# A new hand-written order for gated linear attention and a maxout layer, and four zero fills on another engine

## The chip, the cores and the metric

The kernel runs on one core of one Trainium2 chip, in one launch. The metric is the device time of one execution in microseconds. The engines of the core are TensorE (PE, matrix products and transposes), VectorE (DVE), ScalarE (ACT), GpSimd (POOL) and SyncE (SP, which only issues transfers here).

## The reference

Everything is in float32; the weights come as 64-bit floats. `x`, 3072 x 384, is the result of the attention, and the output has the same shape.

```python
# q, k, v, a_re, a_im: (4, 8, 768, 48), batch x heads x positions x width
mag = sqrt(a_re * a_re + a_im * a_im)
scale = minimum(mag, 0.999) / (mag + 1e-06)
a_re_n, a_im_n = a_re * scale, a_im * scale
for t in range(768):
    new_re = a_re_n[t] * S_re - a_im_n[t] * S_im     # each row of the 48 x 48 state has its decay
    new_im = a_re_n[t] * S_im + a_im_n[t] * S_re
    S_re, S_im = new_re + outer(k[t], v[t]), new_im
    y[t] = q[t] @ S_re
x = y.transpose(0, 2, 1, 3).reshape(3072, 384)
h = maximum(maximum(x @ w1, x @ w2), x @ w3)         # 384 -> 768
out = h @ w_out                                      # 768 -> 384
```

## The kernel before

**Tiles.** The 768 positions are cut into 12 groups of 64 (`g` = 0 to 11). A group holds four batches, as two tiles `x` and `y` of two batches each: 128 partitions and 8 heads x 48 = 384 columns a tile. The products of the decays inside a group are formed as exponentials of summed logarithms and angles, so that a group's attention is a handful of matrix products; only the 48 x 48 states go from a group to the next.

**Stages of a group.** Each stage is a *step*, named `step:g`; where x, y or a digit stands behind the name it is for one tile or one part.
- Loads: `Lr`, `Li` (real and imaginary part of the decay), `Lk`, `Lq`, `Lv`.
- Decay: `sqr` and `sqi` square (ACT), `add` adds (DVE), `lnL`, `expw`, `expe`, `lne`, `relu`, `lnw`, `expL` (ACT), `xor`, `half`, `mulai`, `mulw`, `stt`, `turn` (DVE), `atan` (ACT), the magnitude `abs`, and the additions `Lnop` and `addw`, which from group 1 and 2 on are transfers that add into their destination, issued by POOL. In group 0 these steps are done in two halves (`add0`, `add1`).
- Sums along the group: `cs` and `sums` (PE), then `t`, `nf`, `Cd`, the magnitude `af`, the sines `sa`, `sb`, and the exponentials `En`, `Ek`, `Eq` (ACT).
- Keys and queries: `mk`, `mq`, `uk`, `uq` multiply on DVE into the tiles `uk0` to `uk2` and `uq0`, `uq1` (128 x 8 x 112 columns, of which 16 of each head stay zero); `tpk`, `tpq` are transposes on PE, `Kc`, `Qc` copy their results out of PSUM, `F` and `f0` to `f3` are small factors, `Q1`, `Q2`, `KB`, `QB`, `QG`, `kEn` scale on DVE.
- Scores and state: `A`, `B` (PE), the masked copies `g0` to `g3` (DVE) and `b0`, `b1` (ACT), then `y` (the result) and `dk` (the new state, PE), `h0`, `h1` (DVE), and `xx`, `xy`, which copy the result out.
- The layer behind it: `U11`, `U01`, `U12`, `U02` are products with the three weight matrices (PE, 256 columns for a group), `u11` to `u02` copy or take the maximum; `S`, `P`, `r` and `o` are the product with `w_out` in a form with seven products a pair of blocks, with the product of `w1` and `w_out` folded in; `D` stores.
- Once only: twelve weight blocks, loaded as pairs of integers (`WL`) and decoded to float32 by `Wa` (ACT), `Wb`, `Wc`, `We`, `Wf` (DVE) and `Wg` (an addition); `T`, `t`, `M`, `m` form the folded product; `Zf`, `Zg`, `Zh`, `Z2` to `Z4` and `CL` fill constants.

**The order.** `SCHEDULE` is a list of 1750 such steps, written out by hand, and `run` issues a step's instructions. Nothing is reordered afterwards: `Bound` ties every instruction of an engine behind the one before it on that engine, so the list is each engine's queue, and an instruction that waits holds up all that follow on its engine. The decays of group g+1 or g+2 are thus worked on between the scores of group g and the projection of group g-1. As all instructions are issued through `Bound`, the profile gives them all one line, L198, and they are told apart by the names of their tiles.

**The rooms.** PSUM is used as four rooms of two banks. `SLOTS` is a string of 258 digits: the n-th product that asks for a room gets the one that the n-th digit names, and waits until the reader of the product before it there is done.

**The second engine.** `OTHER` is a set of steps that a second engine does:

```python
def copy(out, in_):          # Kc, Qc, xx, xy: ACT, or DVE
def magnitude(out, in_):     # abs, af: ACT by a table, or DVE by a mask of the bits
def increase(out, in_):      # Lnop, addw, Wg: a POOL transfer that adds, or DVE
(pool if other() else sp).dma_start(...)   # Lk, Lq, Lv: SP's queue, or POOL's
```

and two of the maxima of the layer (`u01`, `u11`) go from ACT to DVE by it.

**The start.** Ahead of the list the first loads are issued and ACT loads its first table of functions. Then ACT fills the parts that stay zero of `uk0`, `uk1`, `uq0` and `uq1`, by multiplying a constant by 0 (lines 1030 and 1031), and DVE those of two `vb` tiles.

Of the kernel before, what the change touches and what calls it, by code (L numbers as in the profile page):

```python
# [22 lines left out]
relu0:0 xor1:0 Lix:1 xor0:0 Lnop0:0 abs0:0 Fx:0 Wa0:0 Wb0:0 half0:0 lnL1:0 expe1:0 expw1:0 lne1:0 Lkx:0 relu1:0 WL3:0
Wc0:0 We0:0 Lnop1:0 Wf0:0 pw0:0 Wa3:0 abs1:0 Wb3:0 half1:0 f3x:0 lnw0:0 Wc3:0 WL6:0 We3:0 f2x:0 expL0:0 mulai0:0 Liy:1
mulw0:0 stt0:0 pw1:0 Lrx:1 Lry:1 f1x:0 Zh:0 Wa6:0 Wb6:0 f0x:0 lnw1:0 expL1:0 mulai1:0 WL9:0 Lqx:0 mulw1:0 sumsx:0
atan0:0 Wf3:0 sqi:1 stt1:0 turn0:0 csx:0 sqr:1 atan1:0 WL10:0 Wc6:0 Eqx:0 tx:0 WL11:0 add:1 We6:0 Wa9:0 turn1:0 Ekx:0
# [10 lines left out]
Lqy:1 mulw:2 We7:0 Cdx:1 WL8:0 U02x:0 b1y:0 u02x:0 Wa8:0 yy:0 xy:0 sb:1 dky:0 stt:2 atan:2 h1y:0 sa:1 Wg5:0 Wf7:0
Wb8:0 U01y:0 turn:2 Wc8:0 mkx:1 U11y:0 u01y:0 u11y:0 U12y:0 Eky:1 Eny:1 mqx:1 ukx:1 U02y:0 Eqy:1 cs:2 sqi:3 uqx:1
tpqx:1 u02y:0 u12y:0 Z2:0 Lvy:1 Wg7:0 Z4:0 tpkx:1 Qcx:1 mqy:1 U21y:0 U21x:0 Lvy:2 u21y:0 We8:0 Wf8:0 Wg8:0 mky:1 Kcx:1
Q1x:1 Q2x:1 U22y:0 sumsx:2 kEnx:1 u22y:0 t:2 u21x:0 nfy:2 uqy:1 Eqx:2 Enx:2 F:2 nfx:2 Ekx:2 Ax:1 tpqy:1 f3:2 f0:2  # L40
uky:1 g0x:1 g1x:1 QBx:1 Oy:0 KBx:1 J3:0 af:2 f2:2 f1:2 Qcy:1 g2x:1 Lqx:2 mqx:2 Lvx:1 tpky:1 Q2y:1 dkx:1 QGx:1 sb:2
g3x:1 sa:2 uqx:2 Q1y:1 Lrx:3 Kcy:1 Bx:1 b1x:1 U12x:0 h0x:1 h1x:1 Lry:3 oy:0 U22x:0 b0x:1 tpqx:2 Lky:2 u12x:0 sqr:3
Qcx:2 KBy:1 Ay:1 QBy:1 u22x:0 sumsy:2 add:3 Lkx:2 g0y:1 g1y:1 g2y:1 g3y:1 Lqy:2 Eky:2 By:1 Lvx:2 yx:1 mky:2 QGy:1
kEny:1 lnL:3 xor:3 expw:3 QBx:2 xx:1 Ox:0 Eqy:2 mkx:2 Lry:4 Dy:0 expe:3 ukx:2 uky:2 b0y:1 Q1x:2 relu:3 Lrx:4 abs:3
lne:3 Lnop:3 addw:3 J1:0 Eny:2 Lqx:3 b1y:1 mqy:2 yy:1 half:3 Cdy:2 Lix:4 Cdx:2 xy:1 Liy:4 lnw:3 expL:3 J2:0 mulai:3
Lkx:3 tpky:2 kEny:2 Kcy:2 tpkx:2 Kcx:2 Lky:3 U11:1 uqy:2 u11:1 mulw:3 U01:1 tpqy:2 stt:3 atan:3 sqr:4 ox:0 h0y:1 dky:1
Q2x:2 turn:3 sqi:4 add:4 KBx:2 sumsx:3 u01:1 Qcy:2 h1y:1 cs:3 Ekx:3 h0y:2 lnL:4 Ax:2 Q2y:2 Enx:3 t:3 relu:4 kEnx:2
g0x:2 Eqx:3 Lix:5 g1x:2 nfy:3 U12:1 g2x:2 nfx:3 u12:1 g3x:2 S3:1 expw:4 U02:1 h0x:2 dky:2 af:3 F:3 expe:4 abs:4 addw:4
mqx:3 sb:3 Q1y:2 u02:1 S1:1 h1y:2 Bx:2 Lqy:3 sa:3 S2:1 Lry:5 Lvy:3 f2:3 Ay:2 b0x:2 g0y:2 P5:1 g1y:2 g2y:2 f0:3 J4:0
QBy:2 S4:1 b1x:2 P1:1 f1:3 f3:3 lnw:4 P7:1 g3y:2 QGx:2 P6:1 r1:1 sumsy:3 KBy:2 expL:4 Dx:0 r6:1 Eky:3 dkx:2 r5:1 r7:1  # L50
r57:1 Eny:3 h1x:2 By:2 yx:2 Lrx:5 xor:4 mkx:3 QGy:2 mky:3 b1y:2 ukx:3 Px:1 lne:4 Lnop:4 Eqy:3 Py:1 mqy:3 mulai:4 h0x:3
P4:1 uqy:3 uqx:3 half:4 Cdx:3 b0y:2 uky:3 P3:1 Lkx:4 Cdy:3 P2:1 xx:2 sqr:5 yy:2 xy:2 tpkx:3 Kcx:3 tpqx:3 Qcx:3 mulw:4
stt:4 U01:2 Lkx:5 Q2x:3 oy:1 Lqy:4 atan:4 Q1x:3 turn:4 ox:1 u01:2 tpky:3 QBx:3 Kcy:3 tpqy:3 F:4 Lqx:4 kEny:3 Qcy:3
QGx:3 Q1y:3 Q2y:3 sumsx:4 cs:4 f3:4 h0y:3 Liy:5 t:4 nfx:4 Ekx:4 Eqx:4 Enx:4 KBx:3 nfy:4 sqi:5 f2:4 U11:2 add:5 Ax:3
Bx:3 f0:4 Dx:1 u11:2 f1:4 lnL:5 g0x:3 mkx:4 Lvy:4 sb:4 Ay:3 mqx:4 g1x:3 af:4 g2x:3 U02:2 g0y:3 sa:4 g1y:3 g3x:3 ukx:4
relu:5 u02:2 g2y:3 Lvx:3 uqx:4 S3:2 g3y:3 KBy:3 U12:2 u12:2 b0x:3 expe:5 expw:5 kEnx:3 Lqx:6 lne:5 tpkx:4 tpqx:4 Lvx:4
dky:3 Kcx:4 S1:2 Qcx:4 dkx:3 Lky:4 sumsy:4 Eqy:4 h1y:3 S2:2 xor:5 Lry:6 Lnop:5 P1:2 Dy:1 abs:5 Eky:4 QBy:3 Lix:6 P7:2
mqy:4 P6:2 b1x:3 h1x:3 addw:5 half:5 Lrx:6 yx:3 mky:4 By:3 Eny:4 uqy:4 Cdx:4 Px:2 Py:2 lnw:5 expL:5 mulai:5 b0y:3
uky:4 Liy:6 P5:2 mulw:5 QGy:3 r1:2 xx:3 r6:2 b1y:3 S4:2 kEnx:4 P4:2 P2:2 r5:2 Cdy:4 sqr:6 sqi:6 P3:2 stt:5 atan:5
tpqy:4 Lqx:5 r7:2 r57:2 add:6 tpky:4 Qcy:4 yy:3 ox:2 dkx:4 Lix:7 Kcy:4 sumsx:5 h0x:4 turn:5 Lrx:7 Dx:2 xor:6 oy:2 xy:3  # L60
h1x:4 Q1y:4 lnL:6 Enx:5 sumsy:5 Eky:5 Ekx:5 Q1x:4 relu:6 mkx:5 cs:5 t:5 U11:3 nfx:5 expw:6 Eqx:5 Q2y:4 nfy:5 expe:6
Lky:5 mky:5 u11:3 abs:6 kEny:4 Eny:5 U01:3 af:5 Q2x:4 half:6 QGx:4 Lry:7 u01:3 Ax:4 Cdy:5 h0y:4 g0x:4 Eqy:5 g1x:4
mqx:5 dky:4 Cdx:5 F:5 g2x:4 U12:3 h1y:4 sb:5 KBx:4 QBx:4 sa:5 uqx:5 Lqy:5 U02:3 f3:5 f2:5 g3x:4 ukx:5 u12:3 uky:5
addw:6 tpqx:5 f0:5 tpky:5 u02:3 lnw:6 expL:6 f1:5 Qcx:5 Ay:4 mulai:6 Bx:4 P1:3 lne:6 Liy:7 S1:3 P5:3 mulw:6 S2:3 b1x:4
Kcy:5 g0y:4 KBy:4 b0x:4 Dy:2 sqi:7 P6:3 QBy:4 g1y:4 g2y:4 g3y:4 By:4 Lvx:5 Lky:6 mqy:5 yx:4 r1:3 S3:3 stt:6 b1y:4 P7:3
uqy:5 atan:6 tpkx:5 b0y:4 tpqy:5 QGy:4 Kcx:5 r6:3 turn:6 yy:4 Qcy:5 r5:3 r7:3 Lnop:6 sqr:7 Q1x:5 xy:4 Lkx:6 Lvy:5
h0x:5 S4:3 Q2y:5 sumsx:6 xx:4 kEnx:5 r57:3 cs:6 t:6 Ekx:6 add:7 nfy:6 Q1y:5 Py:3 nfx:6 lnL:7 P4:3 expw:7 Px:3 U01:4
QGx:5 expe:7 kEny:5 relu:7 Eqx:6 QBx:5 mqx:6 Enx:6 P2:3 af:6 Q2x:5 dkx:5 h1x:5 Liy:8 KBx:5 u01:4 sa:6 mkx:6 abs:7
sumsy:6 Eny:6 F:6 Lry:8 addw:7 oy:3 Lqy:6 U11:4 Eqy:6 P3:3 f2:6 Dy:3 f0:6 h0y:5 Eky:6 f3:6 f1:6 Bx:5 xor:7 u11:4 QBy:5
ox:3 lnw:7 sb:6 Ax:5 KBy:5 Ay:5 mqy:6 By:5 half:7 g0x:5 g1x:5 g2x:5 g3x:5 g0y:5 g1y:5 g2y:5 U02:4 Lvx:6 lne:7 b1x:5  # L70
b0x:5 yx:5 g3y:5 u02:4 expL:7 Lrx:8 mulai:7 U12:4 b1y:5 mulw:7 stt:7 Cdx:6 Lix:8 b0y:5 xx:5 atan:7 ukx:6 S3:4 P7:4
QGy:5 P1:4 tpkx:6 Kcx:6 u12:4 uqx:6 tpqx:6 Cdy:6 yy:5 mky:6 xy:5 S1:4 Qcx:6 S2:4 Dx:3 dky:5 sqi:8 r1:4 turn:7 uky:6
Q1x:6 Lnop:7 sqr:8 h1y:5 add:8 sumsx:7 kEnx:6 cs:7 t:7 P5:4 Eqx:7 P6:4 Px:4 S4:4 Py:4 P4:4 P2:4 Lvx:7 xor:8 Ekx:7
Lkx:7 P3:4 lnL:8 r6:4 uqy:6 nfy:7 r5:4 r7:4 r57:4 nfx:7 expe:8 Enx:7 tpqy:6 tpky:6 h0x:6 Lqx:7 F:7 expw:8 relu:8 mqx:7
af:7 Lvy:6 Lky:8 ox:4 Qcy:6 QBx:6 dkx:6 oy:4 Dy:4 mkx:7 Lix:9 Q2y:6 U11:5 abs:8 Dx:4 QGx:6 half:8 f0:7 Q1y:6 h1x:6
KBx:6 Kcy:6 sb:7 sa:7 f2:7 U01:5 ukx:7 U12:5 Q2x:6 kEny:6 uqx:7 f3:7 addw:8 h0y:6 u01:5 Lrx:9 u11:5 f1:7 u12:5 dky:6
# [988 lines left out]
```

## Time and profile before

| | |
|---|---|
| median of 3 runs | 553.34 us (552.9 to 555.17) |
| the profiled execution: time, span | 549.62 us, 547.9 us |
| mean granted clock of TensorE | 0.983 |
| TensorE busy | 512.3 us (94%), 9998 products |
| VectorE busy | 484.2 us (88%), 730 instructions |
| ScalarE busy | 367.4 us (67%), 575 instructions |
| GpSimd busy | 119.9 us (22%), 173 instructions |
| chain of waits that ended last | PE 72%, DVE 12%, ACT 6%, DMA 4% |

The span runs from the first to the last record of the execution, and its time is 1.7 us longer. The busy times are those of the whole span; a row of the profile that begins with a number gives the start of one instruction in us and how long it took, and what stands in brackets at its end is the idle time of its engine just before, and who ended it. A row with "xN | busy, mean" is a group of like instructions: their count, the busy time of all, the mean of one in ns, and the idle time ahead of them.

### The profile page before, as it was taken

The page shows a single profiled execution, that of the slowest core. Times are in us where ns is not written, and L with a number is a line of the kernel's source. Part 1 is how long each engine was busy: PE and PEld are TensorE (multiplying, and loading weights), DVE is VectorE, ACT ScalarE, POOL GpSimd, SP SyncE. Part 2 cuts the span into 40 slices and gives each one's busy share as a digit, 9 for nine tenths or more (in the row PEclk, how much of TensorE's full clock was granted, in tenths as well). Part 3 has the DMA queues.
Part 4 walks back from the last instruction along what each step waited for, and adds up shares of the span by engine and source line. Part 5 has one row for each costly group of instructions (what it writes and reads, how often), then busy time and mean ns, then how long its engine had stood idle before and what let it go on. Part 6 is the DMA issues. An engine that isn't in the chain of part 4 may idle for free.

```text
span 547.9 us, 22377 instructions
## 1 busy us (share of the span) xinstructions
PE 512.3 (94%) x9998; PEld 439.4 (80%) x9998; DVE 484.2 (88%) x730; ACT 367.4 (67%) x575; POOL 119.9 (22%) x173
## 2 busy tenths in 40 slices
...
GB/s 240 270 203 197 183 155 57 90 91 130 45 76 75 106 81 53 159 63 61 91 21 186 32 17 102 90 67 74 97 68 25 75 105 1 4 44 4 2 0 58
DMA packets 113983, 47.93 MB, mean 87 GB/s; under 512 B 100832, under 2 KB 106400, under 8 KB 113888
## 3 DMA queue, kind: packets, MB, share of 16 engines
...
q8 instruction: 78, 1.28, 1.0%
...
## 4 chain that ended last, share of the span: by engine, by line
PE 72%; DVE 12%; ACT 6%; DMA 4%; issue 3%; SPq 2%; POOL 0%; DVEq 0%; ACTq 0%
PE up L198 28%; PE op L198 22%; PE y L198 6%; PE A L198 4%; PE dk L198 3%; PE tp L198 3%; SPq L198 2%; PE sums L198 2%; DVE xhx L198 2%; ACT L198 2%; PE F L198 1%; PE cs L198 1%; PE B L198 1%; DMA q<-in_q_dram 1%; DVE uk L198 1%
## 5 line engine op out<-in xcount | busy, mean ns | idle before, releaser
L198 PE MATMUL up<-xhx,w 128*128 128x256 f32 x792 | 177.7, 382 | 0.0
L198 PEld LDWEIGHTS up<-xhx,w 128*128 128x128 f32 x792 | 148.4, 190 | 23.4 <-issue 1.2
L198 ACT ACT_TABLE_LOAD x53 | 68.0, 1283 | 4.5 <-issue 3.6
L198 POOL DMA_DIRECT2D ar<-nf x44 | 41.9, 1382 | 85.8 <-DVE ar L198 82.7
L198 PE MATMUL op<-wo,xhx 128*128 128x192 f32 (+1 forms) x220 | 49.2, 362 | 0.0
L198 DVE TENSOR_TENSOR Q<-Q,f 112x1024 f32<-112x1024 f32 (+1 forms) x48 | 44.9, 949 | 0.1
L198 ACT COPY atm<-B 32x128 f32<-32x128 f32 x96 | 24.6, 256 | 29.9 <-DVE atm L198 22.8
L198 PE MATMUL y<-atm,vb 128*32 128x64 f32 x1152 | 39.0, 221 | 0.8 <-issue 0.8
L198 PEld LDWEIGHTS op<-wo,xhx 128*128 128x128 f32 x220 | 36.7, 190 | 3.4 <-ACT xhx L198 0.6
L198 DVE TENSOR_TENSOR xhx<-xhx,up 128x768 f32<-128x768 f32 x22 | 20.9, 950 | 19.7 <-PE up L198 19.6
L198 PEld LDWEIGHTS y<-atm,vb 128*32 128x32 f32 x1152 | 32.9, 109 | 5.0 <-issue 3.1
L198 PE MATMUL y<-QG,g 112*32 112x64 f32 x1408 | 36.7, 218 | 0.0
L198 DVE TENSOR_TENSOR ot<-ot,op 128x192 f32<-128x192 f32 (+1 forms) x66 | 27.1, 416 | 9.7 <-PE op L198 7.0
L198 PEld LDWEIGHTS y<-QG,g 112*32 112x32 f32 x1408 | 34.3, 109 | 0.0
L198 PE MATMUL op<-wo,strassen 128*128 128x192 f32 x176 | 32.9, 330 | 0.0
L198 PE MATMUL op<-w,strassen 128*128 128x192 f32 x176 | 32.5, 329 | 0.3 <-issue 0.3
L198 PE MATMUL A<-Q,K 112*32 112x80 f32 x1536 | 30.8, 234 | 1.4 <-issue 1.3
L198 DVE COPY_PREDICATED atm<-masko,A 128x256 f32<-128x256 uint8 x72 | 30.2, 432 | 1.3
L198 PEld LDWEIGHTS A<-Q,K 112*32 112x32 f32 x1536 | 27.3, 110 | 4.8 <-issue 3.1
L198 ACT ACTIVATE xhx<-up 128x768 f32<-128x768 f32 x16 | 13.0, 811 | 27.0 <-PE up L198 27.0
L198 PEld LDWEIGHTS op<-w,strassen 128*128 128x128 f32 x176 | 29.0, 190 | 2.0 <-issue 1.0
L198 PEld LDWEIGHTS op<-wo,strassen 128*128 128x128 f32 x176 | 28.9, 190 | 1.7 <-ACT e L198 0.6
(155 smaller groups left out, 1116.4 us busy)
## 6 DMA issues: line engine op xcount, KB each, us to landing
...
Ln<-e POOLq DMA_DIRECT2D x11, 384.0 KB, 5.1
...
w<-L POOLq DMA_DIRECT2D x7, 384.0 KB, 4.8
...
```

The lines of the kernel that those rows point to most:

```text
L198: ins = f(*a, **kw)
```

## The change

The four fills of `uk0`, `uk1`, `uq0` and `uq1` go to DVE. The list holds the same 1750 steps in another order, `SLOTS` is another string of as many digits, and `OTHER` holds other steps.

```diff
     for t in us["k"][:2] + us["q"]:
-        act.mul(t[:, :, D:L64], biases[:, 0:1].to_broadcast([P, H * (L64 - D)]).rearrange("p (h d) -> p h d", h=H), 0.0)
+        dve.memset(t[:, :, D:L64], 0.0)
     for t in vbs[:2]:
         dve.memset(t, 0.0)
     program(SCHEDULE, 0)
```

The beginning of the list, and the stretches of group 0's transposes and of `Lnop:2`:

```diff
-Lrx:0 sqr0:0 Lix:0 Zf:0 CL:0 sqi0:0 add0:0 Liy:0 sqi1:0 Zg:0 lnL0:0 Lry:0 WL0:0 sqr1:0 add1:0 expe0:0 expw0:0 lne0:0
+Lrx:0 Lix:0 sqr0:0 Zg:0 CL:0 sqi0:0 add0:0 Liy:0 Lry:0 WL0:0 sqi1:0 xor0:0 lnL0:0 expw0:0 Lix:1 xor1:0 expe0:0 relu0:0
...
-Wc11:0 We10:0 ukx:0 We11:0 uqx:0 lnw:1 T1:0 Lix:2 expL:1 Wf10:0 Wa1:0 Liy:2 Wf11:0 tpqx:0 Qcx:0 mulw:1 Wb1:0 afy:0
-mulai:1 tpkx:0 Wc1:0 t1:0 Fy:0 Kcx:0 kEnx:0 We1:0 WL2:0 Cdy:0 Q2x:0 Eny:0 Wf1:0 Lqx:1 lne:1 f2y:0 Q1x:0 Cdx:0 M0:0
+uqx:0 T1:0 t0:0 lnw:1 tpqx:0 expL:1 Qcx:0 Wf11:0 Lqy:0 Wf10:0 Wa1:0 t1:0 ukx:0 tpkx:0 Fy:0 mulw:1 Kcx:0 Cdx:0 Eqy:0
+f0y:0 f3y:0 lne:1 M0:0 Lky:0 Q2x:0 Q1x:0 WL2:0 Wa2:0 Eny:0 Wb1:0 kEnx:0 Lvx:0 Wc1:0 mulai:1 We1:0 Eky:0 f2y:0 mqy:0
...
-Kcy:0 Enx:1 xx:0 Wf5:0 Q2y:0 U11x:0 Ekx:1 Eqx:1 f2:1 half:2 KBy:0 QBy:0 addw:2 Ay:0 g0y:0 Lnop:2 sumsy:1 g1y:0 f0:1
+Q2y:0 Q1y:0 QBy:0 Zh:0 half:2 F:1 U11x:0 f1:1 WL7:0 Ay:0 WL8:0 Lqx:1 f2:1 f0:1 Ekx:1 KBy:0 Lky:1 lnw:2 u11x:0 Eqx:1
...
+h1y:0 U02y:0 mkx:1 mqx:1 atan:2 turn:2 U11y:0 sa:1 ukx:1 u11y:0 U01y:0 u01y:0 U12y:0 Eqy:1 Eny:1 uqx:1 Wg7:0 Wc8:0
+u12y:0 cs:2 Eky:1 u02y:0 t:2 tpqx:1 We8:0 mqy:1 mky:1 tpkx:1 Wf8:0 Lvx:1 nfx:2 Lky:2 Wg8:0 U21x:0 kEnx:1 Qcx:1 Q1x:1
+Q2x:1 Kcx:1 U21y:0 Lnop:2 u21x:0 u21y:0 U22y:0 u22y:0 sumsx:2 Enx:2 nfy:2 Ekx:2 Lqx:2 uqy:1 F:2 uky:1 KBx:1 Ax:1 g0x:1
```

The second engine's steps that are only in one of the two sets (the loads go between SP's and POOL's queue, the others between ACT or POOL and DVE):

```diff
-Lvy:1 Lkx:2 u11:2 abs:3 Lvy:3 Lky:3 u01:3 u01:5 Lvy:5 xx:6 abs:6 Qcx:6 u01:7 addw:7 Lky:7 Lkx:7 Lqx:8 Lvx:8 af:9 xx:9
-Lvx:9 Lqy:10 Lqx:10 Lvx:10 Lvy:10 xx:10 af:10 Kcx:10 Lkx:11 abs:11 Lvy:11
+Lvx:0 afx:0 Lqx:0 Lky:0 Kcy:1 Lvx:1 Lkx:1 Lqy:2 Lvy:2 Lvx:4 Lqx:4 Lqy:4 Lky:4 Lky:5 Lqy:5 Lqx:6 Kcx:6 af:6 Kcy:6
+u01:6 Lvx:7 Qcy:8 Lvy:8 abs:8 Lkx:8 Lky:8 Qcx:9 Lky:9 u01:10 u11:10 Lky:10 Lnop:11 af:11 Lvx:11 xy:11
```

Instructions that issue transfers go from 126 to 136 on POOL and from 234 to 224 on SP; the stores and all sizes are as they were.

More of the change, by code (lines that the diff above doesn't have):

```diff
@@ L21 @@
 SCHEDULE = """
-Lrx:0 sqr0:0 Lix:0 Zf:0 CL:0 sqi0:0 add0:0 Liy:0 sqi1:0 Zg:0 lnL0:0 Lry:0 WL0:0 sqr1:0 add1:0 expe0:0 expw0:0 lne0:0
[L23 to L26, printed above, removed]
@@ L37 @@
[L37 to L41, printed above, removed]
@@ L42 @@
[L42 to L76, printed above, removed]
@@ new lines @@
+tpqy:1 g1x:1 g2x:1 h0x:1 f2:2 f0:2 Eqx:2 Oy:0 Qcy:1 Q2y:1 af:2 f3:2 Q1y:1 sa:2 mqx:2 tpky:1 f1:2 J3:0 Lvx:2 oy:0 Dy:0
+QBx:1 Kcy:1 sb:2 dkx:1 Bx:1 g3x:1 U22x:0 QGx:1 sqi:3 Lrx:3 Lqx:3 KBy:1 h1x:1 uqx:2 u22x:0 U12x:0 QBy:1 b1x:1 u12x:0
+Ay:1 g0y:1 g1y:1 g2y:1 Lry:3 b0x:1 tpqx:2 By:1 g3y:1 Qcx:2 yx:1 sqr:3 sumsy:2 xor:3 add:3 Eky:2 Lkx:2 lnL:3 mkx:2
+ukx:2 mky:2 expw:3 b0y:1 Lqy:2 Ox:0 b1y:1 Eqy:2 Lvy:2 QGy:1 yy:1 QBx:2 Lrx:4 mqy:2 uky:2 relu:3 expe:3 abs:3 ox:0
+lne:3 J1:0 addw:3 xx:1 tpkx:2 xy:1 half:3 tpky:2 Lix:4 kEny:1 lnw:3 Q1x:2 expL:3 Q2x:2 Kcy:2 mulw:3 J2:0 U11:1 Cdy:2
@@ new lines @@
+r57:1 h1x:2 xor:4 lne:4 half:4 sa:3 Lnop:4 Eky:3 Cdy:3 By:2 b1y:2 b0y:2 Eny:3 yx:2 mkx:3 Py:1 Px:1 Eqy:3 P3:1 P4:1
+ukx:3 QGy:2 yy:2 xy:2 mulw:4 tpkx:3 h0x:3 Lky:4 uqx:3 tpqx:3 oy:1 sqr:5 h0y:3 mky:3 uky:3 mulai:4 xx:2 mqy:3 stt:4
+P2:1 Lkx:4 U01:2 Kcx:3 Qcx:3 uqy:3 sqi:5 Cdx:3 Dy:1 Lqx:4 tpky:3 ox:1 atan:4 KBx:3 turn:4 tpqy:3 u01:2 kEny:3 QGx:3
+sumsx:4 Kcy:3 Qcy:3 Q2y:3 Q1y:3 Q1x:3 Eqx:4 Enx:4 cs:4 F:4 f0:4 QBx:3 t:4 Ekx:4 nfx:4 mqx:4 f3:4 U11:2 Liy:6 f2:4
+u11:2 Q2x:3 f1:4 nfy:4 add:5 sb:4 Ay:3 af:4 g0y:3 Ax:3 Bx:3 xor:5 g0x:3 g1y:3 g2y:3 g1x:3 g2x:3 g3y:3 U02:2 U12:2
@@ new lines @@
+g3x:3 KBy:3 mkx:4 sa:4 lnL:5 ukx:4 expe:5 Lix:6 Dx:1 u02:2 uqx:4 relu:5 Lqy:4 S3:2 Lvx:4 u12:2 Lvy:3 expw:5 abs:5
+tpkx:4 Lqx:6 Kcx:4 kEnx:3 tpqx:4 S1:2 dky:3 Lvx:3 dkx:3 h1y:3 addw:5 Qcx:4 Lry:6 S2:2 b1x:3 sumsy:4 Eky:4 Eqy:4 Eny:4
+P5:2 b0x:3 half:5 Py:2 Cdy:4 lnw:5 P6:2 P1:2 Cdx:4 S4:2 mqy:4 h1x:3 expL:5 QBy:3 lne:5 r1:2 mulw:5 By:3 yx:3 r6:2
+mulai:5 Px:2 P2:2 mky:4 QGy:3 uqy:4 h0x:4 Lnop:5 b1y:3 P7:2 P4:2 r5:2 r7:2 r57:2 Lrx:6 Lvy:4 b0y:3 P3:2 sqr:6 Lvx:5
+xx:3 uky:4 stt:5 tpqy:4 tpky:4 atan:5 Liy:7 Kcy:4 yy:3 oy:2 ox:2 Qcy:4 Dy:2 kEnx:4 kEny:4 sqi:6 turn:5 xy:3 dkx:4
@@ new lines @@
+Lqx:5 add:6 h1x:4 Dx:2 lnL:6 relu:6 Lky:5 sumsx:5 expe:6 QGx:4 sumsy:5 Eqx:5 cs:5 h0y:4 Lkx:5 Ekx:5 Enx:5 mqx:5 Eqy:5
+Q2y:4 Eny:5 mkx:5 U11:3 Eky:5 expw:6 Q1x:4 t:5 Q2x:4 u11:3 lne:6 nfx:5 abs:6 nfy:5 U01:3 u01:3 QBx:4 Ax:4 g0x:4 sb:5
+KBx:4 g1x:4 mky:5 addw:6 dky:4 h1y:4 Lix:7 g2x:4 xor:6 g3x:4 af:5 F:5 sa:5 f1:5 f3:5 half:6 lnw:6 Q1y:4 U12:3 expL:6
+uky:5 uqx:5 f0:5 U02:3 u12:3 mulai:6 f2:5 mulw:6 tpky:5 tpqx:5 Bx:4 u02:3 Ay:4 S1:3 Lnop:6 S2:3 Cdx:5 Lqy:5 Qcx:5
+Kcy:5 stt:6 P1:3 g0y:4 KBy:4 P5:3 g1y:4 b0x:4 Lry:7 P6:3 QBy:4 b1x:4 S3:3 atan:6 Lrx:7 sqr:7 By:4 g2y:4 sqi:7 S4:3
```

123 lines of the change are left out of this document (72 added, 51 removed).

## The prediction

> **What bounds the kernel now.** I read the page's first two parts, then a table of busy time by stretch, then the list of what TensorE (PE) waited for, then single rows around the waits.
>
> ```profile
> span 547.9 us, 22377 instructions
> PE 512.3 (94%) x9998; PEld 439.4 (80%) x9998; DVE 484.2 (88%) x730; ACT 367.4 (67%) x575; POOL 119.9 (22%) x173
> ...
> 0.00:42.00 42.00, 18.42 (x178) 11.62 (x178) 37.40 (x70) 37.56 (x64) 19.93 (x52) 0.83 0.98 238
> 42.00:110.00 68.00, 61.95 (x1315) 47.42 (x1309) 65.36 (x99) 59.08 (x96) 18.60 (x20) 0.98 0.67 134
> 110.00:190.00 80.00, 78.67 (x1600) 66.61 (x1600) 77.93 (x112) 65.09 (x99) 18.01 (x22) 1.00 0.46 86
> 190.00:300.00 110.00, 110.00 (x2344) 97.02 (x2346) 106.10 (x155) 85.18 (x126) 32.72 (x41) 1.00 0.46 89
> 300.00:544.00 244.00, 243.29 (x4589) 216.76 (x4578) 196.06 (x298) 120.51 (x193) 30.67 (x39) 1.00 0.25 49
> 544.00:548.00 4.00, 0.00 (x0) 0.00 (x0) 1.32 (x2) 0.00 (x0) 0.00 (x0) 0.82 0.19 51
> ...
> ```
>
> The stretch rows give the length, then busy us (and instructions) of PE, PE weight loads, VectorE (DVE), ScalarE (ACT) and GpSimd (POOL), then the granted clock and the DMA share. PE is idle for 547.9 - 512.3 = 35.6 us. Of that, 23.6 lie before 42 us, 6.05 between 42 and 110, 1.33 between 110 and 190, none between 190 and 300, 0.71 between 300 and 544, and 4.0 in the tail, which is the last output's addition and store. So from 42 us on the kernel is PE-bound, and until 300 us DVE stands right behind it: idle 2.64 of 68 us, 2.07 of 80 and 3.90 of 110. The matrix products are the same in both kernels, so the time can move by four things only: when PE's unbroken stretch begins, the 8.1 us of gaps inside it, new gaps, and the tail.
>
> The time of this execution was 549.62 us, 1.7 over its span; the median of the runs is 553.34. I work in differences and add them to the median. A difference under 0.5% (2.8 us) is about what a measurement of this kernel cannot tell from none.
>
> **The zero fills.**
>
> ```profile
> 3.62 1.28 ACT L198 ACT_TABLE_LOAD   x1 [3.62 <-issue]
> 4.92 0.51 ACT L198 ACTIVATE uk<-biases 128x128 f32<-128x128 f32 x2
> 5.33 0.49 ACT L198 ACTIVATE uq<-biases 128x128 f32<-128x128 f32 x2
> 5.73 0.51 ACT L198 ACTIVATE e<-ar 128x384 f32<-128x384 f32 x1
> 6.14 0.51 ACT L198 ACTIVATE L<-ai 128x384 f32<-128x384 f32 x1
> 7.08 0.52 ACT L198 ACTIVATE L<-ai 128x384 f32<-128x384 f32 x1 [0.43 <-DMA ai<-in_a_im_dram]
> ...
> 0.99 0.17 DVE L198 MEMSET upto<- 128x128 f32 x1
> 3.23 0.83 DVE L198 MEMSET f<- 32x928 f32 x1 [0.23 <-issue]
> 6.68 0.66 DVE L198 CUSTOM_DVE_ANT_0 L<-L,e 128x384 f32<-128x384 f32 x1 [2.62 <-ACT L L198]
> 7.34 1.09 DVE L198 MEMSET g<- 128x256 f32 x4
> ```
>
> On ACT the four fills take the 0.81 us from 4.92 to 5.73. Without them the first square starts earlier, but the second `ai` square waits for its load until 7.08, with 0.43 us idle before it, and that load does not move. In the new order both `ai` squares still come before everything else of ACT's chain, so the 0.81 us turns into waiting there: worth 0. On DVE a fill of 128x128 took 0.17, so four cost 0.68. They and the 1.09 of `Zg` (which goes ahead of the first addition) total 1.77 and fit the 2.62 us in which DVE waited there for ACT, even if ACT delivers 0.4 sooner. If that cover failed, all DVE steps would be later by at most 0.7. I take 0.
>
> **The start of PE's unbroken stretch.**
>
> ```profile
> 38.41 0.95 DVE L198 SCALAR_TENSOR_TENSOR wo<-w,xhx 128x768 int32<-128x768 int32 x1
> 39.31 0.96 DVE L198 TENSOR_TENSOR w<-pw,L 128x768 f32<-128x768 f32 x1
> 40.32 1.10 PE L198 MATMUL tp<-ident,uk 64*112 64x64 f32 x16 [1.64 <-DVE w L198]
> 42.14 1.65 PE L198 MATMUL wm<-wo,vb 128*128 128x384 f32 x2
> ...
> L198 DVE TENSOR_SCALAR e<-ar 128x384 int32<-128x384 int32 x1 | 0.4, 359 | 0.0
> ...
> ```
>
> Now the transposes `tpkx:0` wait for a PSUM room that DVE's `mulw:1` (39.31 to 40.27) frees, and `M0:0` starts at 42.14. In the new rooms they wait for the copy `Qcx:0` on ACT and for `ukx:0`. `ukx:0` moves behind `uqx:0`, `Wf11:0` and `Wf10:0`, and the magnitude `afx:0` joins DVE: 0.36 by the row of the same bit operation on 384 columns. In DVE's queue that puts the end of `ukx:0` where `Wf11:0` ended (39.36) plus 0.36, hence 39.7; ACT, rid of `afx:0` and with `Wa1:0` behind it, ends `Qcx:0` about then. So this stretch begins some 0.4 us sooner, 0.6 at most. It is a gain only if nothing later takes it back, and the next point does.
>
> **DVE's ledger up to group 3.** PE's last wait before it runs unbroken to 300 us is this one:
>
> ```profile
> 166.64 0.56 PE L198 MATMUL sums<-Ln,mid 64*64 64x192 f32 x8 [0.73 <-DVE ot L198]
> 184.43 2.02 PE L198 MATMUL dk<-vb,uk 64*64 64x48 f32 x126 [0.23 <-DVE xhx L198]
> ...
> L198 DVE COPY K<-tp 112x1024 f32<-112x1024 f32 x5 | 6.1, 1216 | 0.3 <-PE tp L198 0.3
> L198 DVE TENSOR_SCALAR L<-ar 128x768 int32<-128x768 int32 x4 | 2.2, 550 | 0.0
> L198 DVE TENSOR_SCALAR xhx<-up 128x768 f32<-128x768 f32 x6 | 5.6, 946 | 0.0
> L198 DVE SCALAR_TENSOR_TENSOR ai<-ar,ai 128x768 int32<-128x768 int32 x11 | 10.4, 949 | 0.0
> ```
>
> `dky:3` waits for `u12:2`, DVE's maximum at the end of group 2's up-projection. The two orders hold the same DVE steps ahead of `u12:2` but for five. New there: `Kcy:1` (1.22), `afx:0` (0.36) and `xor:5` (0.95). Gone: `abs:3` (0.55) and `u11:2` (0.95), which ACT takes. The sum is 2.53 - 1.50 = +1.03. Since DVE is busy for 143.29 of the 148 us from 42 to 190 (97%), what it has more to do ahead of a step arrives that much later, and PE, which waited there already, waits 1.03 longer. From 190 on PE had no gap at all to 300, so I carry +1.0 to the end. The bounds: the new order could fill all of DVE's idle time from 42 to 190 (2.64 + 2.07 = 4.7) and turn the term into -3.7; or DVE could lose the same time to new waits, +5.7. I take +1.0, as the orders are alike in kind and nothing in the trace names a wait that must appear or go.
>
> ACT's side of these moves: it gains `abs` and maxima and loses copies of K. It is idle 8.9 us from 42 to 110, 14.9 to 190 and 24.8 to 300, which hides them. After 300 us DVE has 48 us of slack, and moves there cost nothing.
>
> **ACT's table loads.** The built orders hold 53 loads of activation tables before and 56 after; up to `atan:4` (about 162 us) it is 16 against 20.
>
> ```profile
> L198 ACT ACT_TABLE_LOAD x53 | 68.0, 1283 | 4.5 <-issue 3.6
> ```
>
> Three more cost 3 x 1.28 = 3.8 us of ACT, the four early ones 5.1. ACT's idle time in the two stretches from 42 to 190 us is 23.8, and the new loads stand where ACT goes from one set of functions to the other and back while it waits for the next product. I take 0 and keep 3.8 for a rival. [...]
>
> **The tail.** The last products, the last addition and the store follow each other as before; the tail's 4.0 us stay. Sum: 0 (fills) + 1.0 (DVE's ledger, which swallows the -0.4) + 0 + 0 = +1.0, hence 553.34 + 1.0 = 554.3 us.
>
> **Rivals.**
>
> *Slower, by ACT.* The extra table loads sit where ACT's idle time is waiting for a product that is itself late, so they are not hidden: the copies K and Q and the halves of the score tiles come later, and PE with them. Price 3.8 on top of +1.0: 558.2 us, +0.9%. For it: four of the loads fall before 165 us, where DVE has no slack to catch up. Against it: ACT's idle time there. It decides from 1.8 us of new PE gaps that ACT ends.
>
> *Slower, by POOL's queue.* These rows carry the case:
>
> ```profile
> Ln<-e POOLq DMA_DIRECT2D x11, 384.0 KB, 5.1
> ...
> 90.05 0.56 PE L198 MATMUL sums<-Ln,mid 64*64 64x192 f32 x8
> ```
>
> `Lnop:2`, the accumulating DMA that `sumsx:2` needs, moves from right behind `addw:2` to behind eleven other entries, `Wg7:0` (which waits for DVE's `Wf7:0`, about 78 us) and `Lvx:1` last. Issued at about 80.5 and landing in 5.1 it is there at 85.6, 4.5 us ahead of `sumsx:2` at 90.05. Should it take 6.5 us longer, PE waits 2.0 more: 556.3 with the forecast's +1.0. From then on every load behind it is later too.
>
> *Faster.* The DVE ledger does not bind because the new order also removes waits: the 0.4 of the start stays, and half of PE's 6.05 us of gaps between 42 and 110 goes. That is -3.4, hence 549.9 us, -0.6%. For it: these gaps are single waits for rooms, which is what new rooms change. Against it: DVE's 2.64 us of idle time there is less than PE's 6.05, so half of them need DVE to be faster, which it is not.
>
> **How the numbers follow.** Forecast (+1.0, own range 551.3 to 556.0, within 0.5%): 0.50. ACT's loads: 0.27, and the POOL queue with what it pushes back: 0.10, at 0.5% or beyond once its followers are counted. Faster: 0.13. So faster 0.13, same 0.50, slower 0.37. The range reaches down to 550.3, which takes in the -3.0 of the faster case that are likeliest, and up to 560.0, past the ACT rival with its own uncertainty of 1.8.
>
> **What would show it.** Right: `dky:3` begins near 185.4 with a wait for DVE, PE's busy total stays at 512 us, and PE's idle sum is 36 to 37. The fills: the first `ai` addition on DVE still ends after 6.2 and ACT still waits for the second `ai`. Wrong: new PE gaps in 190 to 544 us, above all such as ACT or a DMA ends, a stretch that begins later than 43 us, or PE idle under 34.

## The result

The changed kernel takes 556.91 us (median of 20 runs, 550.87 to 562.16); the kernel before, in the same comparison, 551.76 (20 runs, 550.18 to 555.17). The ratio is 1.0067, with a 95% interval of 1.0045 to 1.0089; it leaves out runs more than 1.5% above the fastest of their kernel, six of the changed kernel's (its median without them is 555.95 us) and none of the other's, so it is lower than the ratio of the medians. Slower, then, by 0.7%, where 0.2% was forecast. The profiled execution of the changed kernel took 556.0 us with a span of 554.3, that of the kernel before 549.62 with a span of 547.9.

From the changed kernel's page and the table of stretches, with the columns of the prediction:

```profile
span 554.3 us, 22408 instructions
PE 515.9 (93%) x9998; PEld 440.6 (79%) x9998; DVE 487.4 (88%) x733; ACT 370.3 (67%) x575; POOL 126.0 (23%) x183
...
q8 instruction: 78, 1.28, 1.0%
```

```profile
42.00:110.00 68.00, 62.88 (x1313) 48.02 (x1306) 64.90 (x98) 57.30 (x93) 23.88 (x29) 0.97 0.73 139
110.00:190.00 80.00, 76.21 (x1569) 64.49 (x1570) 76.95 (x109) 69.65 (x100) 18.35 (x23) 0.98 0.43 83
190.00:300.00 110.00, 109.27 (x2248) 95.96 (x2244) 101.70 (x150) 83.25 (x128) 30.58 (x39) 1.00 0.41 80
300.00:544.00 244.00, 242.42 (x4676) 215.18 (x4675) 201.84 (x297) 122.88 (x197) 31.13 (x39) 1.00 0.27 52
```

The span grew by 6.4 us. PE's idle time grew from 35.6 to 38.4 (554.3 - 515.9), by 2.8; but its busy time grew as well, by 3.6, though the products are the same. The loss begins behind 110 us: there PE lacks 3.79 of 80 us where it lacked 1.33, and the clock is 0.98 where it was 1.00. The list of what PE waited for names two kinds of new waits:

```profile
PE y L198 <- issue: 3.0, 2, 1.5
...
PE dk L198 <- issue: 1.2, 1, 1.2
PE tp L198 <- ACT ot L198: 1.2, 1, 1.2
PE up L198 <- ACT xhx L198: 0.9, 1, 0.9
...
PE cs L198 <- issue: 0.6, 1, 0.6
...
PE dk L198 <- DVE xhx L198: 0.3, 1, 0.3
```

**The first kind, near 118 us: ACT, and a half clock behind it.** PE waits 1.16 us for ACT's copy `ox:0` and 0.93 for `xx:1` and `xy:1`. ACT is late since it stood in front of the square `sqr:3`, which waits for group 3's `a_re`; those four transfers went out late, behind the store `Dy:0`, which waits in SP's queue for the copy `oy:0`. The rows of SP's queue, of ACT and of PE in the changed kernel:

```profile
100.47 1.18 SPq L198 DMA_DIRECT2D out_dram<-ot  x2
101.92 4.40 SPq L198 DMA_DIRECT2D ar<-in_a_re_dram  x4
```

```profile
110.38 0.84 ACT L198 ACTIVATE e<-ar 128x768 f32<-128x768 f32 x1 [2.95 <-DMA ar<-in_a_re_dram]
...
118.46 0.46 ACT L198 COPY ot<-op 128x384 f32<-128x384 f32 x1
...
119.65 0.85 ACT L198 COPY xhx<-y 128x384 f32<-128x384 f32 x2
```

```profile
118.97 0.66 PE L198 MATMUL tp<-ident,uk 64*112 64x64 f32 x16 [1.16 <-ACT ot L198]
120.56 3.66 PE L198 MATMUL up<-xhx,w 128*128 128x256 f32 x8 [0.93 <-ACT xhx L198]
```

In the kernel before the same rows read:

```profile
99.90 2.99 SPq L198 DMA_DIRECT2D ar<-in_a_re_dram  x4
```

```profile
105.70 0.84 ACT L198 ACTIVATE e<-ar 128x768 f32<-128x768 f32 x1 [2.27 <-DMA ar<-in_a_re_dram]
```

The square starts 4.7 us later. And PE pays twice. The stretches of the changed kernel, the clock in the third column from the end:

```profile
117.13:120.55 3.42, 1.34 (x40) 1.04 (x32) 3.28 (x5) 3.39 (x7) 0.00 (x0) 1.00 0.68 125
120.55:123.96 3.41, 3.40 (x8) 2.78 (x9) 3.41 (x5) 3.35 (x4) 3.37 (x5) 0.50 0.57 105
123.96:127.38 3.42, 3.42 (x17) 3.01 (x17) 3.39 (x5) 0.97 (x2) 1.13 (x2) 1.00 0.89 160
```

After a stretch of 3.42 us in which PE worked for 1.34, the clock is 0.50 for the next 3.41 us, and 8 products run there where 17 run in the next stretch. That is 1.7 us lost, half of 3.41, which the busy share shows as work. In this trace the clock changes at 21.56, 35.22, 42.04, 45.46, 120.55 and 123.96 us, each time a whole multiple of 3.41 us after the last; such a stretch is called a window below. The one with the half clock came behind a window in which PE was busy for 39%.

**The second kind: gaps in the middle of a step.** Three times PE stops between independent products of one step, with no operand outstanding ("issue"):

```profile
186.56 1.59 PE L198 MATMUL dk<-vb,uk 64*64 64x48 f32 x90 [0.33 <-DVE xhx L198]
189.36 0.73 PE L198 MATMUL dk<-vb,uk 64*48 64x48 f32 x37 [1.21 <-issue]
...
278.67 0.88 PE L198 MATMUL cs<-w,upto 64*64 64x384 f32 x7
280.19 0.53 PE L198 MATMUL cs<-w,upto 64*64 64x384 f32 x1 [0.63 <-issue]
...
433.04 0.88 PE L198 MATMUL F<-cuts,Ln 64*48 64x29 f32 x64
433.85 0.32 PE L198 MATMUL y<-atm,vb 128*32 128x64 f32 x8
433.99 0.29 PE L198 MATMUL y<-QG,g 112*32 112x64 f32 x6
435.80 0.24 PE L198 MATMUL y<-QG,g 112*32 112x64 f32 x1 [1.52 <-issue]
```

The page's queue `q8 instruction` carried 78 packets of 16 KB (1.28 MB / 78). In the trace's records one of them begins at 187.06, one at 277.96 and one at 433.45 us: the three gaps end 2.30, 2.23 and 2.35 us later. The kernel before has one large gap of the kind, in `Ay:0` (a packet at 68.00, the gap's end at 70.23), and these "issue" waits in all:

```profile
PE A L198 <- issue: 1.3, 1, 1.3
PE y L198 <- issue: 0.8, 2, 0.5
...
PE op L198 <- issue: 0.3, 1, 0.3
```

That is 2.4 us by the list, against 5.1 in the changed kernel (3.0 + 1.2 + 0.6 above, and 0.3 for `A`). But not every wait that the list calls "issue" is of this kind. One of the changed kernel's two in `y` is this one:

```profile
75.41 0.88 PE L198 MATMUL y<-atm,vb 128*32 128x64 f32 x48 [1.52 <-issue]
```

It stands at the head of a step, `yy:0`, and ends 0.10 us after ACT's four copies into `atm` (74.25 to 75.31), which `yy:0` reads. In six of the experiments with this order `yy:0` starts 0.10 us after these copies too, whenever they come. By these times it is a wait for ACT, which the list does not name; ACT had stood 1.49 us just before in front of a load of weights. The kernel before's two in `y` are at the head of a step as well, and each ends 0.10 us after a copy of ACT's. The gaps in the middle of a step are thus 1.6 us before (1.26 and 0.32) and 3.6 in the changed kernel (1.21, 0.63, 1.52 and 0.26).

**Where the 6.4 us are.** `dky:3` is PE's 2919th product in both orders, so both executions can be cut there. Up to it the changed kernel needs 2.1 us more (186.56 against 184.43). 3.8 are lost near 120 us, 2.1 by the waits for ACT and 1.7 by the half clock; the rest of that part is 1.7 shorter than before. From it on the changed kernel needs 4.3 us more (367.74 against 363.47). There PE idles 3.85 us instead of 0.80, which is above all the three gaps (3.36), and the same 7080 products keep it busy for 360.0 us instead of 358.9, at full clock in both. What makes them 1.2 us longer is not shown. It belongs to the order: of the profiles without added products, those of the changed order have 360.0 to 360.9, those of the order before 358.9 to 359.1.

### The profile page after: what moved, and what is told of

It reads as the page before. It is cut to its first block, busy times and chain, and to the rows that moved or that the text cites. A ratio compares the mean times of both kernels' runs of the same rounds, so it can differ in the third digit from the quotient of the medians.

```text
span 554.3 us, 22408 instructions
## 1 busy us (share of the span) xinstructions
PE 515.9 (93%) x9998; PEld 440.6 (79%) x9998; DVE 487.4 (88%) x733; ACT 370.3 (67%) x575; POOL 126.0 (23%) x183
## 3 DMA queue, kind: packets, MB, share of 16 engines
q8 instruction: 78, 1.28, 1.0%
## 4 chain that ended last, share of the span: by engine, by line
PE 67%; DVE 7%; ACT 7%; issue 2%; DMA 1%; SPq 1%; DVEq 0%; ACTq 0%
PE up L198 26%; PE op L198 20%; PE y L198 5%; PE A L198 4%; PE dk L198 3%; PE tp L198 3%; PE sums L198 2%; ACT L198 2%; PE B L198 1%; PE F L198 1%; DVE w L198 1%; PE cs L198 1%; ACT L L198 1%; DVE Q L198 1%; DMA ar<-in_a_re_dram 1%
## 5 line engine op out<-in xcount | busy, mean ns | idle before, releaser
L198 PEld LDWEIGHTS up<-xhx,w 128*128 128x128 f32 x792 | 150.0, 191 | 23.8 <-DVE g L198 1.2
L198 POOL DMA_DIRECT2D w<-L x8 | 7.8, 978 | 158.0 <-ACT L L198 46.5
L198 ACT COPY Q<-tp 112x1024 f32<-112x1024 f32 x20 | 20.3, 1017 | 18.6 <-PE tp L198 17.4
L198 DVE TENSOR_TENSOR QG<-Q,f 112x1024 f32<-112x1024 f32 x22 | 26.8, 1220 | 4.9 <-PE y L198 4.9
```

Of the source, the lines that this page charges most:

```text
L198: ins = f(*a, **kw)
```

## The experiments

Each is timed beside the kernel before, which took 550.85 to 552.66 us in these comparisons.

**The store behind the loads.**

```diff
-... J3:0 Lvx:2 oy:0 Dy:0 QBx:1 ... sqi:3 Lrx:3 Lqx:3 ... Lry:3 b0x:1 ...
+... J3:0 Lvx:2 oy:0 QBx:1 ... sqi:3 Lrx:3 Lqx:3 ... Lry:3 Dy:0 b0x:1 ...
```

> The changed kernel with one step moved: the store Dy:0 stands behind the load Lry:3 in SP's queue, not ahead of Lrx:3. Theory of the store: in the changed kernel SP waits with Dy:0 for the copy oy:0, so the four transfers of group 3's a_re go out from 101.9 us on, the last lands at 110.3, ACT stands 2.95 us in front of the square sqr:3 and is late with ox:0, xx:1 and xy:1, and PE idles 1.16 + 0.93 us and then has half its clock for one window of 3.41 us (1.7 us lost). Without the store ahead the loads land some 3 us sooner, those gaps and the half-clock window near 120 us are gone: 3.8 us less than the changed kernel, so about 552 us and level with the kernel before. Theory of ACT's amount of work (abs:3 and four table loads more): the loads come sooner, but ACT is still late at 117 us; 1 us at most is won. Theory of VectorE's ledger (the prediction): no change, 3.7 us over the kernel before.

554.95 us (551.65 to 558.25), ratio 1.0054 [1.0034, 1.0075]. Its ACT rows:

```profile
106.98 0.85 ACT L198 ACTIVATE e<-ar 128x768 f32<-128x768 f32 x1
...
115.52 0.46 ACT L198 COPY ot<-op 128x384 f32<-128x384 f32 x1
...
117.09 0.86 ACT L198 COPY xhx<-y 128x384 f32<-128x384 f32 x2 [0.28 <-PE y L198]
```

The wait for the load, PE's two gaps and the half clock are gone from the profile, though ACT does the same steps, table loads included, in the same order: it is ACT that now waits for PE. So neither ACT's amount of work nor the table loads made it late. In time the gain is smaller than the 3.8 us expected: 0.13% or 0.7 us by the ratios, whose intervals overlap, so the time alone shows none. The profiles tell why it is small. The late load is not in every execution: seven profiles here are of the changed order with the store ahead of the loads. In six of them `sqr:3` waits for its load (2.95 us in the changed kernel, 1.78 to 3.64 in the others), in the seventh, the next experiment's, not at all; in the two with the store behind, never. And its price differs: of the six, only the changed kernel's has a half-clock window near 120 us; in three others PE waits 0.9 to 2.6 us for ACT there, and in the two with half a block of products added not at all.

**The magnitude of group 3 on VectorE.** `abs:3` is added to `OTHER`.

> The changed kernel with abs:3 done by VectorE again, as in the kernel before. Theory of ACT's amount of work: 0.84 us less ahead of ox:0, xx:1 and xy:1 on ACT, so PE's idle time before the window ends falls from 2.1 to about 1.3 us, and the half-clock window may go: 0.8 to 2.5 us less than the changed kernel. Theory of the store: the same, as ACT's queue is shorter by 0.84, but the 2.95 us in front of sqr:3 stay. Theory of VectorE's ledger: VectorE has 0.55 us more ahead of u12:2, so the time is 0.55 us longer.

555.98 us (552.43 to 558.63), ratio 1.0069 [1.0038, 1.0100]. This settles nothing: in its one profile the loads went out in 3.08 us instead of 4.40 and landed in time with the store still ahead, so there was no lateness for the shorter queue to mend. A clear gain or loss from 0.84 us of ACT or 0.55 of VectorE is not to be seen.

**Short products apart.**

```diff
-dky:3 Lvx:3 dkx:3 h1y:3 ... sumsy:4 Eky:4 Eqy:4 Eny:4 P5:2 b0x:3
+dky:3 Lvx:3 h1y:3 ... sumsy:4 Eky:4 Eqy:4 Eny:4 P5:2 dkx:3 b0x:3
...
-dky:5 S2:4 ... sumsx:7 kEnx:6 cs:7 t:7 Q1x:6 QBx:6 P6:4 Py:4
+dky:5 S2:4 ... P6:4 sumsx:7 kEnx:6 cs:7 t:7 Q1x:6 QBx:6 Py:4
...
-F:10 yx:9 QGy:9 ... uqy:10 P5:8 Py:8
+F:10 P5:8 yx:9 QGy:9 ... uqy:10 Py:8
```

A few digits of `SLOTS` are fitted to the moves.

> The changed kernel with three products moved on PE: P5:8 between F:10 and yx:9, P6:4 between dky:5 and sumsx:7, and dkx:3 behind P5:2, away from dky:3. Theory of the instruction stream: PE's gaps in the middle of dkx:3 (1.21 us), cs:7 (0.63) and yx:9 (1.52), which wait for no operand and end 2.2 to 2.4 us after a 16 KB transfer on the instruction queue began, come from many short products in a row that use up the instructions at hand. With a long product between them these three gaps go: 3.3 us less than the changed kernel, unless others open elsewhere. Rival, that these gaps are waits for data or for another engine that the profile does not name: they stay, or move with their steps, and the time stays.

553.06 us (550.57 to 555.98), ratio 1.0029 [1.0011, 1.0048]: 0.38% or 2.1 us less than the changed kernel by the ratios, whose intervals just touch. All three gaps are gone. PE's rows where the first was:

```profile
184.35 1.14 PE L198 MATMUL dk<-vb,uk 64*64 64x48 f32 x64 [0.33 <-DVE xhx L198]
185.60 0.56 PE L198 MATMUL sums<-Ln,mid 64*64 64x192 f32 x8
185.97 0.51 PE L198 MATMUL sums<-Ln,rest 64*64 64x192 f32 x8
186.69 1.57 PE L198 MATMUL op<-wo,strassen 128*128 128x192 f32 x8 [0.21 <-DVE g L198]
188.18 1.14 PE L198 MATMUL dk<-vb,uk 64*64 64x48 f32 x64
```

The rival, that the gaps wait for data, falls: `dkx:3` has the same data and runs through. From `dky:3` on PE idles 1.65 us instead of 3.85, but its products take 360.7 us instead of 360.0, so the profile shows 1.5 us won and not 3.3. It also has two gaps of the kind ahead of all that was moved, 0.99 us in `y` at 65 us and 0.74 in `A` at 70 us, where the changed kernel's own profile has none and 0.26: at the same place a gap is longer or shorter from one execution to the next.

**The store ahead, in the kernel before.**

```diff
-... sa:2 uqx:2 Q1y:1 Lrx:3 Kcy:1 ... Lry:3 oy:0 U22x:0 ... Lry:4 Dy:0 expe:3
+... sa:2 uqx:2 Q1y:1 oy:0 Dy:0 Lrx:3 Kcy:1 ... Lry:3 U22x:0 ... Lry:4 expe:3
```

The copy `oy:0` on ACT moves with its store.

> The kernel before with oy:0 and Dy:0 moved ahead of Lrx:3, as they stand in the changed kernel. Theory of the store: the four transfers of group 3's a_re go out some 1.5 to 2 us later and land up to 4.7 us later than at 105.6; sqr:3, which already stood 2.27 us waiting for them, holds ACT's queue for as much longer, PE idles 2 to 4 us more between 105 and 125 us, and may get a half-clock window (1.7): 2 to 6 us slower than the kernel before. Theories of ACT's amount of work and of VectorE's ledger: no change to the kernel before beyond the 1.4 us of the store's issue, hidden or not.

555.85 us (553.37 to 556.46), ratio 1.0059 [1.0036, 1.0081]: some 3.3 us slower by the ratio. Its rows on SP's queue, ACT and PE:

```profile
102.41 1.18 SPq L198 DMA_DIRECT2D out_dram<-ot  x2
104.25 3.69 SPq L198 DMA_DIRECT2D ar<-in_a_re_dram  x4
```

```profile
110.49 0.84 ACT L198 ACTIVATE e<-ar 128x768 f32<-128x768 f32 x1 [5.42 <-DMA ar<-in_a_re_dram]
```

```profile
112.43 0.32 PE L198 MATMUL y<-atm,vb 128*32 128x64 f32 x8 [2.60 <-ACT Q L198]
```

The square waits 5.42 us where it waited 2.27, PE idles 2.60 us, and from 113.0 to 116.4 us it has half its clock. (A gap of 2.2 us in `Ay:0` stands ahead of the edit and is no part of its price; the profile of the fills alone has one of 2.51 there.) In the profiles the chain from a store's place in SP's queue to PE's clock is thus seen from both sides; in time it is clear in this experiment and not in the first.

**Both edits of the changed kernel together.**

> The changed kernel with both earlier edits: Dy:0 behind Lry:3 in SP's queue, and the three long products between the runs of short ones on PE. If the late loads (with the half-clock window behind them) and the gaps of the instruction stream are two causes of their own, their gains of 2.0 us (554.95 against 556.91) and 3.8 us (553.06 against 556.91) add up: about 551.1 us, level with the kernel before. If the second edit only happened to undo what the first does, the time stays near 553.

553.96 us (550.86 to 557.12) beside 552.66 in that comparison, ratio 1.0021 [0.9995, 1.0047]. From 1.0067 the two single edits took 0.0013 and 0.0038, which would leave 1.0016; the interval takes that in, and no difference from the kernel before remains that can be measured. As far as these runs tell, an order with two local repairs is as good as the old one, though in its profile the products from `dky:3` on still take 2.0 us longer than before (360.9 against 358.9).

**The fills alone, in the kernel before.**

> The kernel before with one part of the change alone: the four zero fills by VectorE. The prediction: 0, as ACT waits for the load of a_im anyway and VectorE has 2.62 us of idle time for 0.68 us of fills; at most +0.7 us. Rival: the ACT chain to the first logarithm is the bound of the start, and 0.8 us are won.

551.85 us (549.79 to 553.99), ratio 0.9977 [0.9954, 1.0000]. The forecast of 0 lies at the edge of the interval. In the profile the second square of `a_im` waits 1.06 us for its load, as forecast.

**Half a block, with the changed kernel's order.**

```diff
+    idle = psum.tile([P, 2, 512], FP, tag="ps0", name="idle")
+    zeros = vbs[0].rearrange("p c i d -> p (c i d)")
+    for _ in range(32):
+        mm(out=idle[:, 0, 0:8], lhsT=zeros[:, 0:P], rhs=zeros[:, 0:8], start=True, stop=True)
     program(SCHEDULE, 0)
```

> The changed kernel, its order untouched, with 32 products of zeros (8 columns each, into a room that nothing has used) ahead of PE's first step, where PE waits some 10 us anyway. They add about 128 instructions to PE's stream, half of a 16 KB block of 256, and so move every later block boundary by half a block against the steps. Theory of the instruction stream with fixed blocks: the gaps in dkx:3, cs:7 and yx:9 shrink or go, others may open in other runs of short products; the time moves by 1 to 3 us, more likely down as three large ones go. Theory that the order alone makes these gaps, wherever the boundaries fall: gaps and time stay within 0.5 us.

580.32 us (579.07 to 581.56), ratio 1.0490 [1.0452, 1.0527]: 23 us slower than the changed kernel, not 1 to 3 us either way. Its list has some twenty gaps by "issue", with 7.9 us for `y`, 4.7 for `F`, 4.5 for `A` and 3.0 for `dk`. But these products took 13.8 us of PE's time at the start, so they were no clean shift.

**The same in the kernel before.**

> The kernel before with the same 32 products of zeros ahead of PE's first step. Theory of the instruction stream with fixed blocks: its one large gap of that kind (1.26 us in Ay:0 at 70.2 us) goes or moves, and others can open at places that had none; the time moves by 1 to 3 us either way, more likely up as it has few. Theory that the order alone makes these gaps: gaps and time stay within 0.5 us.

584.67 us (582.70 to 585.69), ratio 1.0572 [1.0537, 1.0606]. Both orders lose 4 to 6%, with 13.8 us of added products at the start of PE's work in each.

**A whole block, and half a block, of small products.** As above with `lhsT=zeros[0:64, 0:32]` and `rhs=zeros[0:64, 0:8]`, 64 times and 32 times. The profile shows each of them as two products with a weight load each (9998 products become 10126 with 64), so 64 are 256 instructions. That is a 16 KB packet: 9998 products and as many weight loads came in 78 packets, 256 to one.

> The changed kernel with 64 small products of zeros (64x32 by 64x8) ahead of PE's first step: 256 instructions more, which is one whole 16 KB block, so every later block boundary falls at the same step as in the changed kernel. Theory of fixed blocks: the gaps at dkx:3, cs:7 and yx:9 are there as before, no others, and the time is that of the changed kernel (about 557 us) within 2 us for the later start. Rival, that what cost 23 to 32 us in the two kernels with 32 products was the added work or a disturbed start: 575 us or more, and more than the kernel with 32 small products.

> The changed kernel with 32 of the small products ahead of PE's first step: 128 instructions, half a block. Theory of fixed blocks: some 18 gaps of 0.5 to 2 us in runs of short products, as in the kernel with 32 large products, and 575 to 582 us, although there is less added work than in the kernel with 64. Rival (added work or start): between the changed kernel and the kernel with 64.

With 64 products 556.77 us (554.55 to 558.22), ratio 1.0098 [1.0079, 1.0117]; with 32 products 575.91 (573.65 to 578.21), ratio 1.0436 [1.0410, 1.0462]. Half the added work costs 19 us more. PE's waits with 32 products, then with 64:

```profile
PE y L198 <- issue: 7.8, 6, 1.6
PE A L198 <- issue: 4.8, 3, 1.9
PE dk L198 <- issue: 4.5, 4, 1.4
...
PE F L198 <- issue: 4.2, 4, 1.7
```

```profile
PE y L198 <- issue: 1.5, 1, 1.5
...
PE cs L198 <- issue: 1.1, 1, 1.1
...
PE dk L198 <- issue: 0.7, 1, 0.7
```

With a whole block the changed kernel's three gaps are back at their places, and no other of over 0.5 us; the time is 0.3% above the changed kernel's by the ratios, whose intervals overlap. By these two runs (556.77 us with 256 instructions more, 575.91 with 128) what counts is where the boundaries of blocks of 256 instructions fall among the steps. Most boundaries show no gap: the changed kernel has 78 packets and four gaps in the middle of a step, 3.6 us in all.

**Mending the kernel before.** Its large gap stands behind product 45 of the 64 of `Ay:0`.

```diff
-U11x:0 ... Ay:0 g0y:0 Lnop:2 sumsy:1 g1y:0 f0:1 lnw:2 u11x:0 ... g3y:0 Cdy:1 U01x:0 Wc7:0
+U11x:0 ... sumsy:1 U01x:0 Ay:0 g0y:0 Lnop:2 g1y:0 f0:1 u11x:0 lnw:2 ... g3y:0 Cdy:1 Wc7:0
```

`SLOTS` is again fitted to the moves.

> The kernel before with the fills on VectorE and three steps moved: sumsy:1 and U01x:0 ahead of Ay:0 on PE, and u11x:0 ahead of lnw:2 on ACT. In the kernel before, a block boundary falls behind the 45th of the 64 short products of Ay:0, and PE stands 1.26 us there (2.51 in the one profile with the fills on VectorE, where a half-clock window followed). With 56 instructions ahead the boundary comes after 17 products, and the fetch begins in the long products. Theory of fixed blocks: this gap goes, PE idles up to 0.9 us more for yy:0, and half-clock windows near 70 us get rare: 0.5 to 2.5 us less than 551.85. Rival, that the gap belongs to Ay:0: the time stays or grows by 0.9.

553.17 us (551.25 to 554.26), ratio 1.0021 [1.0007, 1.0035]: slower than the fills alone (0.9977), which it was to beat.

```profile
70.54 0.53 PE L198 MATMUL A<-Q,K 112*32 112x80 f32 x17
72.02 0.96 PE L198 MATMUL A<-Q,K 112*32 112x80 f32 x44 [0.95 <-issue]
...
77.79 1.04 PE L198 MATMUL y<-atm,vb 128*32 128x64 f32 x48 [2.92 <-ACT atm L198]
78.76 1.95 PE L198 MATMUL dk<-vb,uk 64*64 64x48 f32 x64
```

The boundary moved from product 45 to product 17, just as reckoned from 56 instructions, which shows that it is fixed in the stream. But the gap only shrank to 0.95, and `yy:0` then waits 2.92 us for its scores, which come later; the clock falls behind it: the 64 products of `dk` from 78.76 us on take 1.95 us, where 64 took 1.14 in the third experiment, and the mean clock from 42 to 110 us is 0.96 where it was 0.98. No version here beats both kernels for certain; the fills on VectorE in the old order come nearest.

**The fills on ScalarE, in the changed kernel.**

> The changed kernel with one part undone: the four zero fills by ScalarE again. The prediction: 0, as ACT waits for the load of a_im in either case (556.9 us, ratio to the kernel before near 1.007). Rival, from the 0.9977 that the fills on VectorE gave in the kernel before: the fills on VectorE are worth up to 0.2%, so the time is about 1.3 us longer, ratio near 1.009.

555.83 us (553.82 to 557.66) beside 550.85, ratio 1.0092 [1.0073, 1.0111], against 1.0067 with them on VectorE. Both comparisons of the fills lean the same way by some 0.2%, and neither is clear by itself.

## Why the prediction came out as it did

The sign was right and the time lay in the range, but not for the reason given: the sum of +1.0 us was made of the wrong term. The range took the time in only because it reached up to 560.0 for the rival by ACT; the forecast's own range ended at 556.0 and 0.5%, and 556.91 and 0.7% came. Of its signs, PE's idle sum was to be 36 to 37 us and was 38.4, and the new gaps behind 190 us were named as a sign of being wrong.

- **What bounds the kernel.** Right that PE does, and that lost time is PE's. Wrong that "the time can move by four things only": with the same products PE's busy total was forecast to stay at 512 us, and it went to 515.9. PE's clock and the length of its products under another order were missing from the list, and its own supply of instructions was not among the causes of new gaps.
- **The fills: 0.** The second `ai` square began at 7.00 us instead of 7.08, with 0.99 us of waiting for its load ahead of it: the time saved turned into waiting, as forecast. The two comparisons leave room for some 0.2% that the rows do not show.
- **The start: 0.4 us sooner.** `tpkx:0` waited for ACT's copy of Q, as forecast, and began at 40.01, 0.3 us sooner.
- **VectorE's ledger: +1.0.** This step failed. VectorE has more to do, though 0.7 us and not 1.03 (busy from 42 us to the end of `u12:2` for 138.35 us instead of 137.66). What was wrong is that a step then comes that much later, for VectorE's idle time up to there is not fixed: it was 4.7 us before, 6.2 in the changed kernel, and 1.9 in the first experiment, which has the same 0.7 us more to do but no loss near 120 us. There `dky:3` begins at 182.34, 2.1 us sooner than before. In the changed kernel it begins at 186.56, later than the 185.4 of the forecast, behind the 3.8 us lost near 120. In each of the three it waits 0.2 to 0.3 us for VectorE.
- **"From 190 on PE had no gap at all to 300, so I carry +1.0 to the end."** The carrying was right: in the first experiment `dky:3` begins 4.2 us sooner than in the changed kernel, and the span is 4.4 us shorter. But 4.3 us were added behind it. The gaps in `cs:7` (280 us) and `yx:9` (436 us) need no late engine: they went when a long product broke the run of short ones, and with the boundaries half a block further on (32 small products added) others came: "issue" waits of 21.3 us by the list in `y`, `A`, `dk` and `F`, which have 4.5 in the changed kernel.
- **The rival by ACT** had the engine and the point of decision: it was to decide from 1.8 us of PE gaps that ACT ends, and 2.1 came near 120 us, besides the 1.52 at 75 us. Its cause was wrong: the table loads and steps stayed in the first experiment, and the gaps went. ACT was late for a load, and the load for a store ahead of it. The prediction looked at POOL's queue alone for such a move; on SP's, the place of `Dy:0` was not priced.
- **POOL's queue** did no harm: `Lnop:2` was issued at 78.25 and had landed at 83.9, and `sumsx:2` began at 90.05, the same as before.

What stays open: why the four loads behind the store sometimes land in time, why a gap at the same block boundary differs in length, what makes the same products 1.2 us longer, and whether the fills are worth 0.2%.
